# Two of four set-aside attention scores computed and copied in halves of 256 queries

## The chip, the cores and the metric

The kernel runs on one core of one Trainium2 chip. The core has five engines with a queue each, which run side by side and wait for one another through semaphores: TensorE (PE; its weight loads are shown as PEld), VectorE (DVE), ScalarE (ACT), GpSimd (POOL) and SyncE (SP, which here only issues transfers). The metric is the device time of one execution in microseconds (us). PE writes its products to PSUM, a small memory in banks of 512 fp32 values a partition; ACT and DVE read them from there.

## The reference

```python
    def _A_ref(x, wqkv, wo):                     # H = 32 heads of Dh = 16, S = 2048, D = 512
        qkv = (lambda x, *d: x.transpose(*d))((x @ wqkv).reshape(B, S, 3, H, Dh), 2, 0, 3, 1, 4)
        q, k, v = qkv[0], qkv[1], qkv[2]
        scores = jnp.einsum("bhqd,bhkd->bhqk", q, k) * Dh ** -0.5
        p = _softmax(scores, axis=-1)
        o = jnp.einsum("bhqk,bhkd->bhqd", p, v)
        return (lambda x, *d: x.transpose(*d))(o, 0, 2, 1, 3).reshape(B, S, D) @ wo
...
    def _B_ref(x, w1, b1, w2, b2):               # F = 1792
        h = jnp.einsum("bsd,df->bsf", x, w1) + b1
        h = jnp.where(h > 0, h, 0) ** 2
        return jnp.einsum("bsf,fd->bsd", h, w2) + b2
...
    xn = _layernorm(x, axis=-1)
    return x + _A_ref(xn, A_wqkv, A_wo) * _silu(_B_ref(xn, B_w1, B_b1, B_w2, B_b2))
```

So: full attention of 32 narrow heads over 2048 positions, a feed-forward with squared ReLU, and their product (through silu) added to the input, all in fp32.

## The kernel before

After some 150 us of layer norm, transposes and the products for keys, queries and values, the kernel runs a loop of 128 turns (line 754). All of the attention lies in it, and the feed-forward and the output projection are cut into single products that fill the gaps.

**Steps.** A step is one quad of heads (8), one block of 512 queries (4) and one block of 128 keys (16): 512 steps, four to a turn, called i to i+3 in turn n with i = 4n. For each step four heads' scores are wanted, [128 keys, 512 queries] each. They are made in two pairs p = 0, 1 of two heads hp = 0, 1. A score is one product (line 282) of 64 rows: hp = 0 uses PE's rows 0 to 63, hp = 1 rows 64 to 127, so two products run side by side. ACT then takes the exponential of a pair at once (1024 columns, line 286), and four products of 32 columns (line 538, `values`) multiply the exponentials with the values and add them up in the bank `acc`. These come at the end of the turn, 16 products x 2 = 32 of the trace's matmuls for the four steps of a turn.

**Two ways to make a score.** PSUM has eight banks. Four of them are two tiles S of two banks each, used by turns: `scores(i, p)` (line 291) makes a pair in one, and ACT reads it from there. Two banks are `spare`, in which the filling products add up; one is `acc`; and one is `single`, named "lin" in the profile, a tile of [128, 512]. For step i+3 the scores are made in `single`, one head after the other, and set aside: `aside(i, p, hp)` (line 300) makes one product and lets DVE copy it to SBUF, into the place of the exponentials (line 305). ACT later takes the exponential from SBUF in place. So a turn has four set-aside scores, (0,0), (0,1), (1,0), (1,1), called first to fourth here, each of which needs `single` again.

**Filling.** `lin(0)` and `lin(1)` (line 339) each issue one product of 64 rows, lower or upper half, for the block in work; `lin(0, 1)` issues both, which run side by side. A set-aside score is paired with one of them: `lin(0)` stands ahead of a score of hp = 1, `lin(1)` behind one of hp = 0. Blocks come in pairs (`pair`), whose two halves are swapped by `swap()` when the one is done. Most pairs take two turns; the first products of the second feed-forward layer, which are short, take one: the turns with `make and end` (line 766), 8 of 128, called two-pair turns here, where `swap()` stands in the middle of the turn.

**Order.** It is written out by hand (the schedule is manual): each engine runs its instructions in the order of the program, and the library adds the semaphores from what each instruction reads and writes. The branch at line 766 is for two-pair turns, the one at 779 for all the others. In both the second and third set-aside scores stand around the pair scores of step i+2.

At the end (lines 827 to 865) the last rows of the output are made; `two` is one of the S tiles there, whose halves `two[:, 0]` and `two[:, 1]` are used apart: `rest(0, ...)` and `end_rest(0, ...)` in the last turn, `rest(1, ...)` at line 847, `end_rest(1, ...)` at line 861, and `lins[3]`, the last group of line 857, is `two[:, 0]` once more.

Of the kernel before, what the change touches and what calls it, by code (L numbers as in the profile page):

```python
# [46 lines left out]
@with_exitstack  # L47
def mha_ffn_kernel(ctx: ExitStack, tc: tile.TileContext, x, wqkv, wo, bx, w1, b1, w2, b2, out):
    nc = tc.nc
    x, out = x[0], out[0]  # L50
    ctx.enter_context(tc.manual_schedule())
    keep = ctx.enter_context(tc.tile_pool(name="keep", bufs=1))
    dram = ctx.enter_context(tc.tile_pool(name="dram", bufs=1, space=DRAM))

    ident = keep.tile([128, 128], FT, name="ident")
    make_identity(nc, ident)
    vt = keep.tile([128, NK, VW], FT, name="vt")
    nvalid = keep.tile([1, 1], I32, name="nvalid")
    stat = keep.tile([128, 80], FT, name="stat")

    kdram = [[dram.tile([128, 2, 1024], FT, name=f"kd{g}_{h}") for h in range(2)] for g in range(4)]
    qdram = [[dram.tile([128, 2, 512], FT, name=f"qd{g}_{c}") for c in range(NC)] for g in range(4)]
    xdram = [dram.tile([128, 2, 4, 512], FT, name=f"xd{c}") for c in range(3)]

    udram = [[dram.tile([2, 2, 16, 4, 512], FT, name=f"ud{g}_{c}") for c in range(NC)] for g in range(4)]
    zdram = [[dram.tile([4, 512], FT, name=f"zd{q}_{c}") for c in range(NC)] for q in range(NQ)]
    gdram = dram.tile([S, D], FT, name="gd")

    with tc.tile_pool(name="sb", bufs=1) as sb, tc.tile_pool(name="ps", bufs=1, space=PSUM) as ps:
        fast_path(tc, sb, ps, locals())  # L70
    general_path(tc, dram, nvalid, ident, vt, kdram, qdram, gdram, x, wo, out)


def fast_path(tc, sb, ps, env):
# [6 lines left out]
    mm = nc.tensor.matmul  # L81
    dve, act, pool, sp = nc.vector, nc.scalar, nc.gpsimd, nc.sync
# [3 lines left out]
    def t(shape, dt, tag):  # L86

        cnt[0] += 1
        p = ps if tag in ("S", "lin", "acc") else sb
        if tag in BUFS:  # L90
            turn[tag] = turn.get(tag, -1) + 1
            n = turn[tag] % BUFS[tag]
            tag = f"{tag}{places[n] if tag == 'S' else n}"
        return p.tile(shape, dt, tag=tag, name=f"{tag}_{cnt[0]}")
# [180 lines left out]
    steps = [(qd, qc, kb) for qd in range(NQ) for qc in range(NC) for kb in range(NK)]  # L275
    ptile = {}

    def score(i, p, hp, dst):
        qd, qc, kb = steps[i]
        k, q = ka[qd, kb // 8], qa[qd, qc]  # L280
        r = slice(64 * hp, 64 * hp + 64)
        mm(dst, k[r, p, 128 * (kb % 8):128 * (kb % 8) + 128], q[r, p], start=True, stop=True)  # L282

    def exps(i, p, src):
        if src is not None:
            act.activation(ptile[i, p], src, AF.Exp, scale=SCALE)  # L286

    def place(i, p):
        ptile[i, p] = t([128, 2, 512], FT, f"P{2 * ((i - 1) % 4) + p}")

    def scores(i, p):

        if i < len(steps):
            sc = t([128, 2, 512], FT, "S")
            place(i, p)
            for hp in range(2):
                score(i, p, hp, sc[:, hp])
            return sc

    def aside(i, p, hp):  # L300

        if hp == 0:
            place(i, p)
        score(i, p, hp, single)
        dve.tensor_copy(ptile[i, p][:, hp], single)  # L305

    gated, complete, gates = {}, set(), set()

# [30 lines left out]
    def lin(*halves):  # L339
        if pair[0]:  # L340
            for half in halves:
                j = half ^ swapped[0]
                pair[0][j].issue(half, lin_banks[j])

    def swap():
        if pair[0]:
            while any([pair[0][half ^ swapped[0]].issue(half, lin_banks[half ^ swapped[0]]) for half in range(2)]):
                pass
            swapped[0] ^= 1
            if not swapped[0]:  # L350
                pair[0][0].evict()
                pair[0] = None
# [21 lines left out]
    def split_piece(eng=None):  # L374
        if at_piece[1] == len(pieces):
            return
        j, layer, m = pieces[at_piece[1]]
        at_piece[1] += 1
        raw, q = raws.pop(0), PAIRS[m][1]
        wf[layer, m] = [t([128, 4, 256] if layer == 1 else [128, 2, 512], FR, f"wf{layer}{p}{q}") for p in "hl"]  # L380
        split(*wf[layer, m], raw, eng or dve, pool)
        load_piece()
# [149 lines left out]
    def values(i):  # L532
        qd, qc, kb = steps[i]
        if kb == 0:
            acc[0] = t([128, 512], FT, "acc")
        for j in (1, 2, 3, 0) if i % 2 else (0, 1, 2, 3):
            o = (4 * qd + j) * 17
            mm(acc[0][32 * j:32 * j + 32], vt[:, kb, o:o + 32], ptile[i, j // 2][:, j % 2],  # L538
               start=kb == 0, stop=kb == NK - 1)

    def finish(i):

        qd, qc, kb = steps[i]
        if kb < NK - 1:
            return
        if i == len(steps) - 1:
            return
        ou = t([128, 512], FT, "ou")
        cast(act if turn_ends_first[0] else dve, ou, acc[0])
        sp.dma_start(zdram[qd][qc], ou[16::32])  # L550
        for j in range(4):
            sp.dma_start(udram[qd // 2][qc][0, qd % 2, :, j], ou[32 * j:32 * j + 16])
        n = i // 4
        events.setdefault(2 * n + 2, []).insert(0, (load_sums, (qd, qc)))
        at(n + 2, rowsums, qd, qc)
# [174 lines left out]
    def happen(time):  # L730
        for fn, a in events.pop(int(2 * time), ()):
            fn(*a)


    n = turn["S"]
# [4 lines left out]
    single = t([128, 512], FT, "lin")  # L740
    xs[0] = xT[3]

    def rest(i, dst):

        group(dst, lambda p: onorm[2, 3][p][:, cut[i]], lambda p: wos[0][p][:, 3])

    def end_rest(i, src):

        o = t([128, 512], FT, f"wf2{'hl'[i // 2]}{i % 2}")
        dve.scalar_tensor_tensor(o, src, 0.5, gsb[2, i // 2][:, i % 2], op0=OP.mult, op1=OP.mult)  # L750
        pool.dma_start(out[1024 + 128 * i:1152 + 128 * i], o, accum_op=OP.add)

    turn_ends_first = [False]
    for n in range(TURNS):
        i = 4 * n
        happen(n)
        make, end, split_now = fill[n]
        if make:
            pair[0] = make()
        exps(i + 1, 0, scores(i + 1, 0))  # L760
        aside(i + 3, 0, 0)
        lin(1)
        exps(i + 1, 1, scores(i + 1, 1))
        for _ in range(5 if make and end else 4):
            lin(0, 1)
        if make and end:
            lin(0)
            aside(i + 3, 0, 1)
            exps(i + 2, 0, scores(i + 2, 0))
            swap()  # L770
            exps(i + 2, 1, scores(i + 2, 1))
            aside(i + 3, 1, 0)
            lin(1)
            exps(i + 3, 0, ptile[i + 3, 0])
            lin(0, 1)
            last = [scores(i + 4, 0)]
            for _ in range(4):
                lin(0, 1)
        else:
            lin(0)  # L780
            aside(i + 3, 0, 1)
            exps(i + 2, 0, scores(i + 2, 0))
            lin(0, 1)
            lin(0, 1)
            exps(i + 2, 1, scores(i + 2, 1))
            aside(i + 3, 1, 0)
            lin(1)
            exps(i + 3, 0, ptile[i + 3, 0])
            lin(0, 1)
            lin(0, 1)  # L790
            last = [scores(i + 4, 0)]
            lin(0, 1)
            lin(0, 1)
        lin(0)
        aside(i + 3, 1, 1)
        exps(i + 3, 1, ptile[i + 3, 1])
        last.append(scores(i + 4, 1))
        for p in range(2):
            exps(i + 4, p, last[p])
        if n == TURNS - 1:  # L800
            two = t([128, 2, 512], FT, "S")
            rest(0, two[:, 0])
        turn_ends_first[0] = n < LAST and end and fill[n][0] is None and fill[n - 1][2] and n % per in (7, 15, 23)
        swap()
        if n == LAST - 1:
            gsb.update({(2, i): y[2, i] for i in range(2)})
        if n == TURNS - 1:
            end_rest(0, two[:, 0])
        happen(n + 0.5)
        if split_now:  # L810
            split_piece()
        for j in range(4):
            values(i + j)
        finish(i + 3)
# [5 lines left out]
    zc, r = t([128, 16], FT, "zc"), t([128, 16], FT, "rc")  # L820
# [15 lines left out]
    for i in range(4):  # L836
        for j in range(4):
            mm(small[32 * j:32 * j + 32, 0, cut[i]], r[:, 4 * i + j:4 * i + j + 1].broadcast_to([128, 32]), ident,
               start=True, stop=True)
# [138 lines left out]
```

## Time and profile before

| | |
|---|---|
| three runs | 1273.32 us (median), 1272.75 to 1273.88 |
| profiled execution, own time | 1272.96 us |
| its span, first to last instruction | 1271.1 us |
| granted TensorE clock | 0.998 |
| PE, PEld, DVE, ACT, POOL busy | 1257.3, 721.4, 678.5, 1034.2, 257.8 us |
| set-aside products (line 282 into "lin") | 512 |
| their copies (line 305) | 512, 692 ns each |

How to read the lines that follow: the page counts an engine as busy while an instruction of its runs, but PE's matmuls are pipelined and their ends modelled, so 99% is no statement about its peak. A group's line gives the line of the kernel, the engine, the operation, the tiles written <- read (without their numbers), how often, the time in all and the mean in ns; behind the second bar stands how long the engine was idle just before and for whom. The chain of waits follows the work that ended last back from the end; in order of time each piece has its start, its length and what it was. In the timeline a bracket at the end of a row gives the idle time before it and what ended it.

### The profile page before, as it was taken

What the parts mean: (1) busy time and instruction counts of PE and PEld (TensorE: products, weight loads), DVE (VectorE), ACT (ScalarE), POOL (GpSimd) and SP (SyncE); (2) the same over time, 40 slices, a digit from 0 to 9 for tenths busy, and PEclk for the clock granted to TensorE, in tenths of its full rate; (3) what the DMA queues carried; (4) which work ended last, traced back from release to release, by engine and by line L of the source; (5) the groups of instructions that cost most, each with busy time, mean ns of one, the idle gap of its engine ahead of it and who ended that gap; (6) DMA issues with size and microseconds to landing.
All of it is one profiled execution on the core that took longest, in us unless ns stands there. A gap on an engine that the chain in (4) does not pass through costs nothing.

```text
span 1271.1 us, 24788 instructions
## 1 busy us (share of the span) xinstructions
PE 1257.3 (99%) x9925; PEld 721.4 (57%) x9925; DVE 678.5 (53%) x1065; ACT 1034.2 (81%) x1123; POOL 257.8 (20%) x149
## 2 busy tenths in 40 slices
PE   9999999999999999999999999999999999999996
PEld 7888755555555455555555555555555555545553
DVE  5542255455555654545465455555554545566655
ACT  4222588889899898898988889899889988998883
POOL 5000122122211221312022221220331212322111
PEclk9999999999999999999999999999999999999999
DMA  7565513131233132121423222333222132463445
GB/s 266 206 232 197 217 43 102 58 93 59 77 125 109 59 105 64 45 87 48 152 73 109 60 76 60 93 125 108 58 60 87 47 89 59 142 216 125 143 129 118
DMA packets 84940, 137.32 MB, mean 108 GB/s; under 512 B 26058, under 2 KB 40408, under 8 KB 83284
## 3 DMA queue, kind: packets, MB, share of 16 engines
q1 hardware_dynamic: 81668, 126.25, 30.9%
q0 software_dynamic: 2720, 8.65, 2.3%
q8 instruction: 79, 1.29, 0.4%
q10 hardware_dynamic: 432, 0.79, 0.2%
q14 instruction: 41, 0.34, 0.1%
HBM read 94.24 MB, written 41.41 MB: 107 GB/s over the span
## 4 chain that ended last, share of the span: by engine, by line
PE 96%; DVE 2%; ACT 1%; POOL 0%; DMA 0%; issue 0%; ACTq 0%; DVEq 0%
PE acc L538 36%; PE spare L330 26%; PE S L282 16%; PE S L111 9%; PE lin L282 7%; DVE P L305 1%; PE S L204 1%; POOL hl L104 0%; DMA P<-in_A_x_dram 0%; PE acc L111 0%; DVE st L166 0%; DVE P L858 0%; ACT P L286 0%; DVE P L864 0%; ACT wf2h L98 0%
## 5 line engine op out<-in xcount | busy, mean ns | idle before, releaser
L286 ACT ACTIVATE P<-S 128x1024 f32<-128x1024 f32 x768 | 732.4, 1020 | 67.9 <-PE S L282 64.5
L305 DVE COPY P<-lin 128x512 f32<-128x512 f32 x512 | 354.1, 692 | 467.6 <-PE lin L282 342.7
L538 PE MATMUL acc<-P,vt 128*32 128x512 f32 x4096 | 466.0, 595 | 0.0
L282 PE MATMUL S<-QA,KA 64*128 64x512 f32 x1536 | 332.8, 422 | 0.1
L286 ACT ACTIVATE P<-P 128x1024 f32<-128x1024 f32 x256 | 271.4, 1060 | 43.7 <-DVE P L305 43.6
L538 PEld LDWEIGHTS acc<-P,vt 128*32 128x32 f32 x4096 | 120.2, 110 | 272.9 <-issue 272.9
L282 PEld LDWEIGHTS S<-QA,KA 64*128 64x128 f32 x1536 | 145.3, 184 | 159.9 <-ACT P L286 142.6
L282 PE MATMUL lin<-QA,KA 64*128 64x512 f32 x512 | 213.2, 416 | 1.0 <-DVE P L305 0.3
L104 POOL TENSOR_TENSOR wf1l<-wr,wf1h 128x1024 fp32r<-128x1024 f32 x28 | 66.8, 2384 | 404.5 <-DVE wf1h L100 135.3
L330 PE MATMUL spare<-xl,wf1h 64*128 64x512 f32 x504 | 122.3, 400 | 0.0
L104 POOL TENSOR_TENSOR hl<-T,hh 128x1024 fp32r<-128x1024 f32 x28 | 67.6, 2415 | 242.2 <-PE S L282 131.3
L104 POOL TENSOR_TENSOR wf2l<-wr,wf2h 128x1024 fp32r<-128x1024 f32 x28 | 66.7, 2383 | 207.4 <-PE acc L538 139.1
L330 PE MATMUL spare<-wf2l,hh 64*128 64x512 f32 x448 | 107.1, 399 | 0.0
L282 PEld LDWEIGHTS lin<-QA,KA 64*128 64x128 f32 x512 | 94.2, 184 | 22.3 <-DVE P L305 13.6
L330 PE MATMUL spare<-xh,wf1l 64*128 64x512 f32 x504 | 96.3, 392 | 0.0
L330 PE MATMUL spare<-xh,wf1h 64*128 64x512 f32 x504 | 95.5, 390 | 0.0
L330 PE MATMUL spare<-wf2h,hh 64*128 64x512 f32 x448 | 87.7, 392 | 0.0
L330 PE MATMUL spare<-wf2h,hl 64*128 64x512 f32 x448 | 84.6, 391 | 0.0
L330 PEld LDWEIGHTS spare<-xl,wf1h 64*128 64x128 f32 x504 | 67.0, 185 | 8.2
L330 PEld LDWEIGHTS spare<-xh,wf1h 64*128 64x128 f32 x504 | 60.0, 185 | 9.8
L330 PEld LDWEIGHTS spare<-xh,wf1l 64*128 64x128 f32 x504 | 59.8, 185 | 8.4
L98 ACT CAST P<-S 128x512 fp32r<-128x512 f32 x30 | 17.6, 587 | 57.7 <-PE S L111 55.9
(201 smaller groups left out, 995.6 us busy)
## 6 DMA issues: line engine op xcount, KB each, us to landing
wr<-in_B_w_dram SPq DMA_DIRECT2D x56, 512.0 KB
KA<-kd SPq DMA_DIRECT2D x64, 256.0 KB
QA<-qd SPq DMA_DIRECT2D x128, 128.0 KB
kd<-P SPq DMA_DIRECT2D x15, 512.0 KB
qd<-P SPq DMA_DIRECT2D x15, 512.0 KB
u<-ud SPq DMA_DIRECT2D x15, 512.0 KB
P<-in_A_x_dram SPq DMA_DIRECT2D x8, 512.0 KB
xd<-KA SPq DMA_DIRECT2D x4, 1024.0 KB
```

Source lines behind the costliest of these rows:

```text
L98: act.copy(dst, src)
L104: leng.tensor_tensor(lo, src, hi.bitcast(FT), op=OP.subtract)
L111: mm(dst, lhs(a, k), rhs(b, k), start=n == 0, stop=n == len(todo) - 1)
L204: nc.tensor.transpose(pt[:, k, 128 * j:128 * j + 128], xnorm[c, i][:, j, 128 * k:128 * k + 128], ident)
L282: mm(dst, k[r, p, 128 * (kb % 8):128 * (kb % 8) + 128], q[r, p], start=True, stop=True)
L286: act.activation(ptile[i, p], src, AF.Exp, scale=SCALE)
L305: dve.tensor_copy(ptile[i, p][:, hp], single)
L330: mm(bank, self.lhs(a, k)[r], self.rhs(b, k)[r], start=n == 0 and self.at[other] == 0, stop=n == len(self.todo[half]) - 1 and self.at[othe ...
L538: mm(acc[0][32 * j:32 * j + 32], vt[:, kb, o:o + 32], ptile[i, j // 2][:, j % 2], start=kb == 0, stop=kb == NK - 1)
```

## The change

The function `score` gets the columns of the queries as an argument, and `aside_half` makes and copies 256 of the 512 queries of one set-aside score, in the matching half of `single`. The second set-aside score (0,1) is made as two such halves, one right behind the other, in all turns. The third (1,0) is made as two halves too: in ordinary turns the second half stands behind `lin(1)`, in two-pair turns behind `lin(1)` and two `lin(0, 1)`, one of which stood behind ACT's exponential and the other behind `scores(i + 4, 0)`. The first and the fourth stay whole.

```diff
-    def score(i, p, hp, dst):
+    def score(i, p, hp, dst, cols=slice(0, 512)):
         qd, qc, kb = steps[i]
         k, q = ka[qd, kb // 8], qa[qd, qc]
         r = slice(64 * hp, 64 * hp + 64)
-        mm(dst, k[r, p, 128 * (kb % 8):128 * (kb % 8) + 128], q[r, p], start=True, stop=True)
+        mm(dst, k[r, p, 128 * (kb % 8):128 * (kb % 8) + 128], q[r, p, cols], start=True, stop=True)
...
+    def aside_half(i, p, hp, n):
+
+        if hp == n == 0:
+            place(i, p)
+        s = slice(256 * n, 256 * n + 256)
+        score(i, p, hp, single[:, s], s)
+        dve.tensor_copy(ptile[i, p][:, hp, s], single[:, s])
...
         if make and end:
             lin(0)
-            aside(i + 3, 0, 1)
+            for m in range(2):
+                aside_half(i + 3, 0, 1, m)
             exps(i + 2, 0, scores(i + 2, 0))
             swap()
             exps(i + 2, 1, scores(i + 2, 1))
-            aside(i + 3, 1, 0)
+            aside_half(i + 3, 1, 0, 0)
             lin(1)
+            lin(0, 1)
+            lin(0, 1)
+            aside_half(i + 3, 1, 0, 1)
             exps(i + 3, 0, ptile[i + 3, 0])
-            lin(0, 1)
             last = [scores(i + 4, 0)]
-            for _ in range(4):
+            for _ in range(3):
                 lin(0, 1)
         else:
             lin(0)
-            aside(i + 3, 0, 1)
+            for m in range(2):
+                aside_half(i + 3, 0, 1, m)
             exps(i + 2, 0, scores(i + 2, 0))
             lin(0, 1)
             lin(0, 1)
             exps(i + 2, 1, scores(i + 2, 1))
-            aside(i + 3, 1, 0)
+            aside_half(i + 3, 1, 0, 0)
             lin(1)
+            aside_half(i + 3, 1, 0, 1)
             exps(i + 3, 0, ptile[i + 3, 0])
```

## The prediction

> **What bounds the kernel now.** I read the page first: busy times, then the chain that ended last, then the costliest groups.
>
> ```profile
> PE 1257.3 (99%) x9925; PEld 721.4 (57%) x9925; DVE 678.5 (53%) x1065; ACT 1034.2 (81%) x1123; POOL 257.8 (20%) x149
> PE 96%; DVE 2%; ACT 1%; POOL 0%; DMA 0%; issue 0%; ACTq 0%; DVEq 0%
> L286 ACT ACTIVATE P<-S 128x1024 f32<-128x1024 f32 x768 | 732.4, 1020 | 67.9 <-PE S L282 64.5
> L305 DVE COPY P<-lin 128x512 f32<-128x512 f32 x512 | 354.1, 692 | 467.6 <-PE lin L282 342.7
> L538 PE MATMUL acc<-P,vt 128*32 128x512 f32 x4096 | 466.0, 595 | 0.0
> ```
>
> TensorE is the bound: 96% of the chain is its own work. DVE and ACT have room, but what they do counts where PE waits for it. The 4096 value products, 32 a turn, say that there are 128 turns. The next view is the chain of waits inside two of them, in order of time. An ordinary turn (from its second set-aside score on):
>
> ```profile
> 408.36 0.43 PE S L282 x2
> ...
> 410.18 0.23 PE lin L282
> 410.41 0.23 PE S L282 x2
> 410.64 0.46 PE spare L330 x4
> 411.11 0.28 PE S L282 x2
> 411.39 0.33 PE lin L282
> 411.72 0.47 PE spare L330 x5
> ...
> 413.13 0.23 PE S L282 x2
> 413.36 3.57 PE acc L538 x32
> 416.93 0.42 PE S L282
> ```
>
> And a turn in which two output blocks of the feed-forward share the filling (a two-pair turn):
>
> ```profile
> 425.48 0.43 PE S L282 x2
> ...
> 427.53 0.23 PE lin L282
> ...
> 427.84 0.70 DVE P L305
> ...
> 428.58 0.50 PE lin L282
> ...
> 430.84 0.24 PE S L282 x2
> ...
> 434.64 0.42 PE S L282
> ```
>
> A slot, two products side by side in the two halves of PE's rows, takes 0.23 us. The ordinary turn lasts 416.93 - 408.36 = 8.57 us, and PE loses only some 0.15 in it: 0.28 - 0.23 at S, 0.33 - 0.23 at the third set-aside score. The two-pair turn lasts 434.64 - 425.48 = 9.16, and there DVE's copy of the second set-aside score stands in the chain, since the third one's product must wait for the same bank. By the code only 8 of the 128 turns are of this kind (one pair of blocks each, four query blocks of two). So all that the change can win there is 8 x (9.16 - 8.57) = 4.7 us, while it edits two products in all 128 turns.
>
> **The change part by part.** It removes, per turn, two 512-column products into `single` and their two copies, and puts four 256-column products and four 256-column copies in their place. No DMA moves, and nothing is moved past SP's or POOL's queue; ACT's order stays. In two-pair turns one filling slot moves ahead of S(i+4, 0), and the third score's second half stands behind three slots. What decides is one question: `single` is one 128x512 tile; does a product into one half of it wait until DVE has read the other half? The order in program is product, copy, product, copy, so such a wait would put a whole round trip between the halves. The trace has no 256-column piece of this tile, but at the kernel's end two halves of another PSUM tile, `two`, are handled apart: line 861 reads `two[:, 1]` (through line 750), the last group of line 857 then writes `two[:, 0]`, which nobody had read since the last turn. The timeline there, and beside it the chain, where pieces of 256 columns in SBUF go from DVE to ACT:
>
> ```profile
> 1259.94 0.67 DVE L750 SCALAR_TENSOR_TENSOR wf2h<-S,y 128x512 f32<-128x512 f32 x1
> 1260.66 0.30 PEld L664 LDWEIGHTS S<-QA,wf1h 128*128 128x128 f32 x2 [0.56 <-DVE wf2h L750]
> ```
> ```profile
> 1257.05 0.44 DVE P L849
> ...
> 1257.56 0.41 ACT wf1h L850
> ```
>
> PE had nothing else to wait for, and yet it stood 0.56 us until DVE had read the other half: 1259.94 + 0.67 = 1260.61, and 0.05 later it began. In SBUF that isn't so: ACT began the first half at 1257.56 while DVE's second (two of 0.42, row below) was still running. For a tile in PSUM I take the first reading: the halves wait for each other's copies.
>
> The Trainium skill bears on this, in "PSUM — Partial Sum Buffer", section "PSUM bank collisions raise a hardware error": PE may not write a bank and quadrant of partitions while another engine reads it, whatever the columns, so the guard goes by bank. By that rule the two 256-column halves, in one bank of 512, must wait for each other, while `two`'s halves, in two banks, need not; the row shows a wait even there. The rule and the row give the same sum here; the rule speaks against the change.
>
> Price of one round trip, from these rows of the timeline and of the groups:
>
> ```profile
> 408.89 3.80 ACT L286 ACTIVATE P<-S 128x1024 f32<-128x1024 f32 x4 [0.59 <-PE S L282]
> 410.02 0.39 PE L282 MATMUL lin<-QA,KA 64*128 64x512 f32 x1
> 410.48 0.69 DVE L305 COPY P<-lin 128x512 f32<-128x512 f32 x1 [0.66 <-PE lin L282]
> 411.23 0.49 PE L282 MATMUL lin<-QA,KA 64*128 64x512 f32 x1
> ```
> ```profile
> L849 DVE TENSOR_TENSOR P<-S,P 128x256 f32<-128x256 f32 x2 | 0.8, 420 | 1.0 <-PE lin L846 1.0
> L833 DVE COPY zc<-lin 128x16 f32<-128x16 f32 x1 | 0.2, 175 | 0.1
> L282 PEld LDWEIGHTS lin<-QA,KA 64*128 64x128 f32 x512 | 94.2, 184 | 22.3 <-DVE P L305 13.6
> ```
>
> - From product to copy: 410.48 - 410.02 = 0.46 for 512 columns. Half a slot less for 256 (0.46 - 0.115) is 0.35, which I take; the upper end is 0.46.
> - The copy: 692 ns at 512 columns, 175 at 16, so about 0.43 on the line between at 256; line 849 at 256 has 0.42, which I take. The lower end is half of 692, 0.35.
> - From the copy's end (410.48 + 0.69 = 411.17) to PE: 0.06, and 0.05 at `two`. I take 0.05.
> - A product that had to wait shows 0.49 to 0.50 where one that didn't shows 0.39: it streams some 0.11 after its wait is over. The lower end is nothing.
>
> The second half thus streams 0.35 + 0.42 + 0.05 + 0.11 = 0.93 us after the first (0.75 to 1.04). One filling product runs beside the first half; then PE, which issues in order, has everything queued behind the waiting half: S(i+2, 0), the filling, S(i+2, 1). ACT and DVE wait for them in turn.
>
> An ordinary turn by hand, from its second set-aside score as 0. Before, S(i+2, 0) came at 0.23; now it goes beside the second half at 0.93: +0.70. Two filling slots and S(i+2, 1) follow, so PE is at the third score's first half at 0.93 + 4 x 0.23 = 1.85. It needs the copy of the second score's second half, which ends at 0.93 + 0.35 + 0.42 = 1.70, plus 0.05: no new wait, by 0.10. Then comes the second stall of 0.93, and the half behind it takes half a slot to a weight load, 0.115 to 0.184, say 0.13: 0.93 + 0.13 - 0.23 = +0.83. The old 0.15 of waits is covered. Sum +1.38, a turn of 9.95 us. Nothing absorbs it: the eight exponentials at 1.02 make about 8.2 us, they start some 0.55 after their S product as before (408.89 against 408.36), and the two S tiles are free again long before they are wanted; the 3.57 of value products ends the turn as before. DVE has one fixed cost more per split copy, 2 x 0.42 - 0.69 = 0.15, but it stands idle there.
>
> A two-pair turn: half two at 0.93, with it S(i+2, 0), then S(i+2, 1) at 1.16. The third's first half waits for the copy, 1.75 + 0.11 = 1.86 (before, 428.58 + 0.11 - 427.53 = 1.16). Three filling slots, 0.69, don't cover 0.93: the second half at 2.79, S(i+4, 0) at 2.92, three slots and the fourth score, S(i+4, 1) at 4.07 against 430.84 - 427.53 = 3.31 before. +0.76.
>
> Sum: 120 x 1.38 + 8 x 0.76 = 165.6 + 6.1 = 171.7; less some 2 us, an estimate, for the output projections at the end that have 9 instead of 12 products per half and so leave PE room: +170. The profiled execution took 1272.96 us (span 1271.1), the median of the runs is 1273.32, the same within 0.03%: 1272.96 + 170 = **1443 us**. With 0.75 for the round trip a turn costs 1.38 - 2 x 0.18 = 1.02, in all +126: 1399. With 1.04 the third's first half also waits: it comes at 1.04 + 0.92 = 1.96, the copy is done at 1.04 + 0.46 + 0.42 + 0.05 = 1.97, which costs a restart; 1.38 + 2 x 0.11 + 0.12 = 1.72 a turn, in all some +213: 1486.
>
> **The rivals.**
>
> 1. *The halves are kept apart, and it helps.* If a product waits only for its own 256 columns, the third's first half may start when the second's first half is copied, 0.35 + 0.42 + 0.05 = 0.82 after the second score, before PE gets there in an ordinary turn. The 0.10 at 411.39 goes, and at best the whole 0.59 of the two-pair turns: 120 x 0.10 + 8 x 0.59 = 16.7, so 1256 us. For it speaks SBUF, where pieces are kept apart (1257.56); against it the 0.56 us before 1260.66. It decides as soon as nothing waits for the other half.
> 2. *Kept apart, but the weights cost.* Each half loads its own weights: the row says 184 ns, the half streams 115. Two such halves in the same rows need 0.37 instead of 0.23, +0.14 twice a turn: 120 x (0.28 - 0.10) = 21.6, less some 3 in two-pair turns: 1292 us. Between 1 and 2 it may come out even.
> 3. *The stalls chain.* The margin of 0.10 ahead of the third's first half is thin: where DVE is late by more than that, a third wait is added, as worked out above: 1486 or a little more.
>
> That the change doesn't do what it says is my forecast itself: the halves are there, but the second product can't run ahead of the first copy.
>
> The Trainium skill has another figure for rival 2: "TensorE: Matmul & The Clock Gate", section "LDWEIGHTS (loading the stationary operand)", gives columns over 1.2 GHz, 107 ns for 128. By that a load would hide under a half's 115 and rival 2 would cost nothing; the row's 184 decides. My own sum would go down by 0.015 a turn, under 2 us.
>
> **How the numbers follow.** Forecast 0.83; rival 1, 0.06; rival 2, 0.04; an even outcome between them, 0.03; rival 3, 0.04. The time is the forecast's, 1443; the range, 1400 to 1486, is what the bounds of the round trip make it, and takes in rival 3; 0.13 is left out. This kernel's runs can tell 0.2%, 2.5 us, from no change: faster 0.06, same 0.03, slower 0.91.
>
> **What would show it.** In the profile after: four copies of 128x256 at about 0.42 us a turn beside two of 128x512; a turn of some 9.95 us; in the chain DVE's copies twice in every turn, about 256 x 0.42 = 108 us, some 7% of the span; waits of PE on these copies some 256 times, 0.6 us each, where before they came to 13.6 us in all. PE's granted clock stays. I am wrong if a second half's product starts before the first half's copy has ended, or if the turn stays near 8.6 us.

## The result, and the profile after

The changed kernel takes 1461.99 us (median of four runs, 1461.70 to 1462.64) against 1273.49 before (four runs): **1.148 times as long**, 95% interval 1.1466 to 1.1495. The profiled execution took 1462.08 us, its span is 1460.3, the granted clock 0.997. The forecast was 1443 (1400 to 1486).

The page of the changed kernel, its busy times, chain and the groups that are new. Line 313 is the copy in `aside_half`, line 546 the value products:

```profile
PE 1328.5 (91%) x10181; PEld 773.1 (53%) x10181; DVE 718.8 (49%) x1321; ACT 1044.9 (72%) x1123; POOL 257.4 (18%) x149
PE 88%; DVE 9%; issue 2%; POOL 0%; DMA 0%; ACT 0%; DVEq 0%; ACTq 0%
L313 DVE COPY P<-lin 128x256 f32<-128x256 f32 x512 | 217.5, 425 | 283.8 <-PE lin L282 171.4
L282 PEld LDWEIGHTS lin<-QA,KA 64*128 64x128 f32 x768 | 141.0, 184 | 226.3 <-DVE P L313 222.1
```

DVE, 2% of the chain before, is 9% of it now, and what PE's weight loads wait for DVE's copies has gone from 13.6 us to 222.1. DVE's own work rose by only 40 us (678.5 to 718.8). Who waited for whom says it in counts (us in all, times, longest):

```profile
PEld lin L282 <- DVE P L313: 222.1, 268, 1.0
```

268 times is 2 x 128, and a few more. The chain shows where. First an ordinary turn, then a two-pair turn, each from one set of value products to the next:

```profile
458.99 3.57 PE acc L546 x32
462.56 0.43 PE S L282
...
464.69 0.43 DVE P L313
465.12 0.04 issue
465.17 0.38 PE lin L282
...
466.62 0.44 DVE P L313
467.06 0.04 issue
467.10 0.38 PE lin L282
...
469.10 3.57 PE acc L546 x32
```
```profile
475.02 0.44 DVE P L313
475.45 0.04 issue
475.50 0.40 PE lin L282
475.89 0.02 issue
475.91 0.44 DVE P L313
476.35 0.04 issue
476.39 0.38 PE lin L282
476.78 0.58 PE spare L338 x5
...
479.13 3.57 PE acc L546 x32
```

An ordinary turn lasts 469.10 - 458.99 = 10.11 us (8.57 before), with DVE's copy of a half in the chain twice. In the two-pair turn, 479.13 - 469.10 = 10.03 us (9.16 before), the third score's first half waits as well (475.91), and its second half, with three filling slots ahead of it, hardly does. Over all turns, from one turn's first value product to the next's, the mean is 10.09 us in ordinary and 10.05 in two-pair turns (8.58 and 9.15 before): 120 x 1.51 + 8 x 0.90 = 188 us, the whole of the change. The timeline shows one round trip close up. The columns are start, duration, engine, line and operation; the bracket is the idle time before:

```profile
444.03 0.28 PE L282 MATMUL lin<-QA,KA 64*128 64x256 f32 x1
...
444.47 0.42 DVE L313 COPY P<-lin 128x256 f32<-128x256 f32 x1 [0.66 <-PE spare L338]
444.95 0.18 PEld L282 LDWEIGHTS lin<-QA,KA 64*128 64x128 f32 x1 [0.90 <-DVE P L313]
444.95 0.38 PE L282 MATMUL lin<-QA,KA 64*128 64x256 f32 x1 [0.55 <-DVE P L313]
...
445.37 0.42 DVE L313 COPY P<-lin 128x256 f32<-128x256 f32 x1 [0.47 <-PE lin L282]
445.99 0.28 PE L282 MATMUL lin<-QA,KA 64*128 64x256 f32 x1
...
446.40 0.42 DVE L313 COPY P<-lin 128x256 f32<-128x256 f32 x1 [0.60 <-PE lin L282]
446.88 0.18 PEld L282 LDWEIGHTS lin<-QA,KA 64*128 64x128 f32 x1 [0.82 <-DVE P L313]
```

The second half's weights load at 444.95, not before: the copy of the first half ends at 444.47 + 0.42 = 444.89, and 0.06 later PE goes on. PE stood idle 0.55 us: the one filling product that ran beside the first half had ended before that.

### The profile page after: what moved, and what is told of

Read it like the earlier page. It is cut to its first block, busy times and chain, and to the rows that moved or that the text cites. A ratio compares the mean times of both kernels' runs of the same rounds, so it can differ in the third digit from the quotient of the medians.

```text
span 1460.3 us, 25556 instructions
## 1 busy us (share of the span) xinstructions
PE 1328.5 (91%) x10181; PEld 773.1 (53%) x10181; DVE 718.8 (49%) x1321; ACT 1044.9 (72%) x1123; POOL 257.4 (18%) x149
## 4 chain that ended last, share of the span: by engine, by line
PE 88%; DVE 9%; issue 2%; POOL 0%; DMA 0%; ACT 0%; DVEq 0%; ACTq 0%
PE acc L546 31%; PE spare L338 23%; PE S L282 14%; PE lin L282 10%; PE S L111 8%; DVE P L313 8%; PE S L204 0%; POOL hl L104 0%; DMA P<-in_A_x_dram 0%; PE acc L111 0%; DVEq L313 0%; DVE st L166 0%; DVE P L871 0%; POOL wf2l L104 0%; DVE P L877 0%
## 5 line engine op out<-in xcount | busy, mean ns | idle before, releaser
L282 PE MATMUL S<-QA,KA 64*128 64x512 f32 x1536 | 386.5, 418 | 0.0
L282 PE MATMUL lin<-QA,KA 64*128 64x256 f32 (+1 forms) x768 | 271.2, 353 | 117.2 <-DVE P L313 116.7
L313 DVE COPY P<-lin 128x256 f32<-128x256 f32 x512 | 217.5, 425 | 283.8 <-PE lin L282 171.4
L305 DVE COPY P<-lin 128x512 f32<-128x512 f32 x256 | 177.0, 691 | 333.4 <-PE lin L282 212.5
L282 PEld LDWEIGHTS lin<-QA,KA 64*128 64x128 f32 x768 | 141.0, 184 | 226.3 <-DVE P L313 222.1
L282 PEld LDWEIGHTS S<-QA,KA 64*128 64x128 f32 x1536 | 197.8, 184 | 113.4 <-ACT P L286 106.5
L338 PE MATMUL spare<-xh,wf1l 64*128 64x512 f32 x504 | 115.5, 403 | 0.0
L338 PE MATMUL spare<-wf2h,hl 64*128 64x512 f32 x448 | 98.9, 401 | 0.0
L338 PEld LDWEIGHTS spare<-xl,wf1h 64*128 64x128 f32 x504 | 79.5, 185 | 3.5
L338 PEld LDWEIGHTS spare<-wf2l,hh 64*128 64x128 f32 x448 | 70.7, 185 | 2.7
```

The lines of the kernel that those rows point to most:

```text
L313: dve.tensor_copy(ptile[i, p][:, hp, s], single[:, s])
L338: mm(bank, self.lhs(a, k)[r], self.rhs(b, k)[r], start=n == 0 and self.at[other] == 0, stop=n == len(self.todo[half]) - 1 and self.at[othe ...
```

## The experiments

Theory: the halves of one PSUM tile are guarded as one, so each half after the first costs a round trip from PE to DVE and back. Rivals: the second weight load and product, the doubled copies, or a guard that would let the halves pass in another cut. All runs were made beside the kernel before, which took 1273.4 to 1274.2 us there. Unless rounds are told of, a time is that of one run.

### Each split alone

Against the changed kernel, the second alone in halves (in two-pair turns the filling goes back to its places too), then the third alone:

```diff
-            aside_half(i + 3, 1, 0, 0)
+            aside(i + 3, 1, 0)
             lin(1)
-            aside_half(i + 3, 1, 0, 1)
```
```diff
-            for m in range(2):
-                aside_half(i + 3, 0, 1, m)
+            aside(i + 3, 0, 1)
```

> Only the second set-aside score is in halves, the third is whole as before. Theory (a half's product waits for the copy of the half before it, one round trip of 0.9 us a split score): +0.70 for the stall, +0.1 for rows left uneven, less the 0.15 of waits that stand there now: +0.65 a turn, 1273 + 128 x 0.65 = 1356 us. Rival (two products of half the width cost what they cost because each loads its own weights): half of the change's 188, 1367 us, but with no wait on the copy between the halves in the trace.

> Only the third set-aside score is in halves, the second is whole as before. Theory: +0.83 for the stall and some 0.05 for uneven rows, and the small wait ahead of the third's first product stays: +0.85 a turn, 1382 us; with the run of the second alone the two add up to the change's 188 within 15. Rival (weight loads): 1367.

Measured: 1377.59 us and 1375.57 us, +103 and +101 against 1274.17 beside them. The second took 22 us more than expected, the third 6 less; together they make 205, 16 more than the change's 188.5, so "within 15" was just missed. Both show the wait (118.6 us in 136 and 99.6 us in 132 for the weight loads, against 222.1 in 268), so the two stalls are of like size. The times alone don't tell the theory from the rival; the next run does. What the 16 us are isn't shown. Where they lie depends on what one counts from. On the mean over the ordinary turns, from the first product of the pair S(i+4, 0) to the value products it is 1.36 us with the second alone, 1.35 with the third alone, 1.35 with both and 1.27 before, as if 0.08 were lost once, however many scores are split; from the pair's second product it is 1.31, 1.23, 1.23 and 1.25, and no such loss is seen.

### The same products, copied whole

Against the kernel before, with `score` as in the change:

```diff
     def aside(i, p, hp):
...
-        score(i, p, hp, single)
+        if p == hp:
+            score(i, p, hp, single)
+        else:
+            for n in range(2):
+                c = slice(256 * n, 256 * n + 256)
+                score(i, p, hp, single[:, c], c)
         dve.tensor_copy(ptile[i, p][:, hp], single)
```

> The second and third score are made by two products of 256 columns each, one right behind the other, but copied whole, in one copy of 512; all places as before the change. The weight loads and the extra products are those of the change, the round trip between the halves is gone. Theory: uneven rows of 0.1 to 0.15 per split score, partly hidden: 1273 + 128 x (0 to 0.3) = 1273 to 1310 us, no wait on a copy between the halves. Rival (weight loads and extra products are the cost): near the changed kernel, 1440 or more.

Measured: 1273.19 us, where the kernel before took 1274.17. The 768 products into "lin" with their 768 weight loads are all there, as in the changed kernel, and cost nothing that a single run would show; their waits for copies are 6.6 us in all:

```profile
L282 PEld LDWEIGHTS lin<-QA,KA 64*128 64x128 f32 x768 | 129.0, 184 | 21.2 <-DVE P L310 6.6
```

This is the run that decides: take only the copy from between the halves, and 188 us are gone. Rival 2 of the prediction falls, weights and all.

### The same copies, of a whole product

Against the kernel before:

```diff
         score(i, p, hp, single)
-        dve.tensor_copy(ptile[i, p][:, hp], single)
+        for c in ([slice(0, 512)] if p == hp else [slice(0, 256), slice(256, 512)]):
+            dve.tensor_copy(ptile[i, p][:, hp, c], single[:, c])
```

> The kernel before with whole products, but DVE copies the second and third score in two copies of 256 columns each. DVE's part of the change alone, with no product between the copies. Theory: the two copies take 0.85 instead of 0.69 us, so what waits for them waits up to 0.16 longer, at the third score and at ACT's last exponentials: 0 to 0.16 a turn, 1273 to 1295 us. Rival (the doubled copies are the cost): most of the 188 us.

Measured: 1282.47 us, +9 against 1273.42. First a two-pair turn, then an ordinary one, and who waited in all:

```profile
438.59 0.28 PE lin L282
...
438.89 0.77 DVE P L306 x2
```
```profile
457.04 0.29 PE S L282 x2
457.34 0.39 PE lin L282
```
```profile
PEld lin L282 <- DVE P L306: 30.2, 127, 0.7
```

The two copies take 0.77 together where one took 0.70 (427.84). The two-pair turn had that copy in its chain before, and these turns are no longer than they were (9.15 us on the mean). An ordinary turn's chain has no copy in it; there the third score, whose weights wait a little longer for the pair of copies (30.2 us in all, before 13.6), stands 0.39 in the chain where it stood 0.33 (411.39), and 120 times the 0.06 are 7 of the 9 us.

So neither the products alone (0) nor the copies alone (9) make the 188; their order, product, copy, product, copy, does.

### How coarse the guard is: halves by keys

Against the changed kernel (`score` takes 64 keys instead of 256 queries):

```diff
+        if keys < 128:
+            kw, qw = kw.bitcast(FT), qw.bitcast(FT)
...
-        s = slice(256 * n, 256 * n + 256)
-        score(i, p, hp, single[:, s], s)
-        dve.tensor_copy(ptile[i, p][:, hp, s], single[:, s])
+        s = slice(64 * n, 64 * n + 64)
+        score(i, p, hp, single[s], 64 * n, 64)
+        dve.tensor_copy(ptile[i, p][s, hp], single[s])
```

> The same places as in the changed kernel, but the halves are 64 keys by 512 queries: they lie on different partitions (0 to 63, 64 to 127) of the bank instead of different columns. Their products run in plain fp32, which takes two passes, 0.45 us a half instead of 0.115, and each copy is 64x512, about 0.69. It tells how coarse the wait is. Theory that the whole tile is guarded: the second half's product starts only after the first's copy has ended, a round trip of some 1.5 us, twice a turn: near 1700 us. Rival that the guard goes by the bank and its partitions: the second half follows the first at once, while the first is being copied; only the dearer products count, some +1.35 a turn, near 1445 us.

Measured: 2113.02 us, above both. Its timeline:

```profile
620.84 1.07 PE L285 MATMUL lin<-QA,KA 64*64 64x512 f32 x2
621.94 0.68 DVE L316 COPY P<-lin 64x512 f32<-64x512 f32 x1 [1.63 <-PE lin L285]
622.68 0.19 PEld L285 LDWEIGHTS lin<-QA,KA 64*64 64x64 f32 x2 [1.66 <-DVE P L316]
622.68 1.07 PE L285 MATMUL lin<-QA,KA 64*64 64x512 f32 x2 [0.78 <-DVE P L316]
```

The time is no measure: a half's product took 1.07 us, not the 0.45 that I had put in. The order is: the second half, on other partitions, began at 622.68, 0.06 after the first's copy had ended (621.94 + 0.68). So the guard isn't one by partitions either. With the wait at `two`, whose halves are in different banks, this says that in this kernel a PSUM tile is guarded as a whole, by the semaphores that the library adds. Whether the chip itself would allow such an overlap wasn't tried: there was no ninth bank to give the halves tiles of their own.

### The round trip's terms: what stands ahead of the half, and what stands behind it

Against the changed kernel, the filling product behind the second score's first half (in both kinds of turns), then two more slots between the third's halves (in ordinary turns):

```diff
-            lin(0)
-            for m in range(2):
-                aside_half(i + 3, 0, 1, m)
+            aside_half(i + 3, 0, 1, 0)
+            lin(0)
+            aside_half(i + 3, 0, 1, 1)
```
```diff
             aside_half(i + 3, 1, 0, 0)
             lin(1)
+            lin(0, 1)
+            lin(0, 1)
             aside_half(i + 3, 1, 0, 1)
             exps(i + 3, 0, ptile[i + 3, 0])
-            lin(0, 1)
-            lin(0, 1)
```

> The changed kernel with the filling product lin(0) of the second score issued behind its first half instead of ahead of it; nothing else differs. In the changed kernel the first half's copy starts 0.44 us after the product, not the 0.35 of the prediction. Theory: the half's end is held by the 512-column product ahead of it on PE; now that is gone, the copy starts 0.35 after, 0.09 a turn less: 1462 - 11 = 1451 us. Rival (the time from product to copy doesn't depend on the columns or the neighbour): 1462, still 0.44.

Measured: 1445.12 us, 17 less than the changed kernel's 1462 where 11 were expected. The half and its copy:

```profile
440.10 0.27 PE L282 MATMUL lin<-QA,KA 64*128 64x256 f32 x1
440.41 0.42 DVE L313 COPY P<-lin 128x256 f32<-128x256 f32 x1 [0.52 <-PE lin L282]
```

0.31 us from the product to its copy, where the changed kernel has 0.44 and names the filling product ("PE spare") as what the copy waited for. So the half's end was held by the 512-column product issued just ahead of it.

> The changed kernel, but in ordinary turns too the third score's second half stands behind lin(1) and both lin(0, 1), as the change has it in two-pair turns. No work is added or taken. Theory (the cost is a round trip in which PE only stands still, so work placed into it is free): 0.46 of the third's 0.93 is filled; the fourth score then comes 0.82 after the second half and must wait some 0.1 to 0.2 for its copy, so 0.26 to 0.46 a turn are saved: 1407 to 1431 us. Rival (the cost is work on PE or DVE): 1462.

Measured: 1418.79 us, in the range: 43 less with the same work in another order. Time that can be filled with other work was waiting, not work. In the chain the second stall is gone:

```profile
436.29 0.70 PE spare L338 x5
436.99 0.30 PE lin L282
437.29 0.23 PE S L282 x2
```

### More pieces

> Only the second score by two products of 256 columns, copied whole; the third by one. Both split scores together cost nothing when copied whole (1273), while each alone as halves cost more (103 and 101 us) than half of the two together (188). Theory: two products in one half of PE's rows leave it some 0.1 us behind the other half; the second does that to the rows 64 to 127, the third to the rows 0 to 63, so together they are even and alone they aren't: 128 x (0.06 to 0.13), 1281 to 1290 us. Rival (the rows don't matter): 1273.

The edit is that of the run with whole copies, for the second score alone. Measured: 1271.89 us against 1273.66, in three rounds, ratio 0.9988 (0.9979 to 0.9998): two products in one half of the rows cost nothing when they are copied whole, and with that my theory for the 16 us falls. What causes them stays open.

Last, the second score alone in quarters, against the run with it alone in halves:

```diff
-            for m in range(2):
+            for m in range(4):
                 aside_half(i + 3, 0, 1, m)
...
-        s = slice(256 * n, 256 * n + 256)
+        s = slice(128 * n, 128 * n + 128)
```

> Only the second score, in four quarters of 128 queries, each copied by itself; the third whole. Theory (every piece after the first adds one round trip): the first takes 0.42 to its copy, about 0.29 for a copy of 128 columns (on the line through 175 ns at 16 and 425 at 256) and 0.05, in all 0.76; the two behind it 0.11 + 0.25 + 0.29 + 0.05 = 0.70 each; the last streams 0.11 after its wait: 2.27 us from the first product to S(i+2, 0), against 1.03 with halves. +1.24 a turn over the run with the second alone in halves, 1378 + 159 = 1536 us. Rival (the cost goes by the columns handled apart, which are the same 512): 1378.

Measured: 1589.11 us, 53 above. Its chain, an ordinary turn:

```profile
456.32 3.57 PE acc L546 x32
...
461.99 0.30 DVE P L313
462.33 0.34 PE lin L282
462.70 0.30 DVE P L313
...
463.04 0.34 PE lin L282
463.40 0.30 DVE P L313
...
463.75 0.33 PE lin L282
...
466.96 3.57 PE acc L546 x32
```

Three copies in the chain, 0.71 apart (462.33, 463.04, 463.75 against the 0.70 worked out), and a turn of 10.64 us; with the second score in halves it is 9.39, so +1.25 against the +1.24 expected. The price of a round trip holds; the 53 us come from something else, the last section.

### A better order?

Against the kernel before, in ordinary turns:

```diff
-            lin(0, 1)
-            lin(0, 1)
+            for _ in range(3):
+                lin(0, 1)
             exps(i + 2, 1, scores(i + 2, 1))
             aside(i + 3, 1, 0)
             lin(1)
             exps(i + 3, 0, ptile[i + 3, 0])
-            lin(0, 1)
             lin(0, 1)
```

> Not the change but the kernel before, all scores whole; in ordinary turns one lin(0, 1) moves from behind the third score to ahead of S(i+2, 1). By the trace of before PE loses 0.05 at S(i+2, 1) and 0.10 at the third score of such a turn. Theory: both waits are covered, and the fourth score, whose copy of the third must be done by then, costs back 0.1 at most: 120 x (0 to 0.15), 1256 to 1274 us. Rival (the exponentials bound the turn too, ACT is just as late): 1273, the same.

Measured: 1275.80 us against 1273.42 in five rounds, ratio 1.0018 (1.0009 to 1.0027): no gain. The third score's wait is gone (PE's weight loads waited 6.2 us for copies, before 13.6), and an ordinary turn takes 8.61 us on the mean, before 8.58. So the 0.10 at the third score was no loss that a better place would win back. The wait has moved to S(i+4, 0), which now comes sooner than ACT has freed its tile:

```profile
412.18 0.19 PEld L282 LDWEIGHTS S<-QA,KA 64*128 64x128 f32 x2 [0.23 <-ACT P L286]
```

It waits so in all 118 ordinary turns between the first and the last of the loop, in the kernel before in 9 of them, while S(i+2, 1) waited for ACT in 115 there. That is what the rival said: the exponentials are just as late. None of the runs beats the kernel before by more than 0.2%.

## Why the prediction was right

- **The bound, and what can be won.** Right: PE sets the turn, and the stall of the two-pair turns is a small target. It wasn't even won: these turns grew from 9.15 to 10.05 us.
- **The decisive reading.** Right, and shown: from the wait at `two` the prediction took it that halves of a PSUM tile wait for each other's copies. Whole copies (1273), the timeline (444.95) and the halves by keys all say the same. The Trainium skill's "PSUM — Partial Sum Buffer", section "PSUM bank collisions raise a hardware error", forbids the overlap in one bank and quadrant; the guard seen here is coarser than that rule, as it also held between partitions 0 to 63 and 64 to 127.
- **The round trip.** 0.93 forecast. Copy 0.425 (0.42 forecast), copy to PE 0.06 (0.05), restart 0.10 to 0.11 (0.11): right. From product to copy I had 0.35; it is 0.31 with nothing in the way (440.10 to 440.41, and 0.42 after a restart), but 0.44 and 0.41 in the changed kernel. This term was mis-sized: I subtracted half a slot for the shorter product and forgot that it comes behind a long one (shown for the 0.44; for the 0.41 it wasn't tried apart). 0.09 + 0.06 = 0.15 a turn.
- **An ordinary turn.** +1.38 forecast, 10.11 - 8.57 = +1.54 in the turn shown. The mean is +1.53 up to the last 16 turns and +1.40 in those, which have the output projections; 16 x 0.13 are the 2 us that the forecast took off there. The 0.15 make up the difference; that the third score's first half wouldn't wait, by a margin of 0.10, held (445.99 has no bracket). Not all of the old 0.15 of waits was covered: S(i+2, 1) still takes 0.28 in the chain (466.25).
- **A two-pair turn.** +0.76 forecast, +0.87 measured in the turn shown, +0.90 on the mean. The third's first half waits as forecast (475.91); that the rest is the same term is argued, not shown.
- **The sum.** 1443 forecast, 1462 measured: 120 x 0.15 = 18 us of the 19 missing.
- **Rival 1** (the halves are free of each other) never came about, since nothing passes the guard. **Rival 2** costs nothing that the runs show: a weight load that the row gives 184 ns is hidden although the half streams for 115, both alone (1271.9) and for both scores (1273.2). **Rival 3** didn't come: a third wait is seen in the 8 two-pair turns only, where the forecast itself had it.
- **What would show it.** Two copies in the chain of each turn, 256 waits and an unchanged clock came as said; the waits were longer or shorter than the 0.6 us each, by what one counts: 222 us by the weight loads (0.83 each, of which part passes beside the neighbour's product), 117 by the products (0.47).

## What to carry to other kernels

Cutting a piece of work in two to free its buffer earlier can help only if the halves are tracked apart; where the buffer is guarded as one, each cut adds a whole round trip between the engines, product to copy to product, and the engine that issues in order stands still for all of it that isn't filled with other work. Look for a place in the trace where two parts of such a buffer are already used apart, and read there whether anyone waited. And count the turns: a stall in 8 of 128 doesn't pay for an edit in all.

## What was not expected of the hardware

PE's clock. In the changed kernel, which pauses twice a turn, and in all others but two it was granted in full over the whole loop (0.997 or 0.998 over the span). With three pauses in a row (the quarters) it was halved in the loop 33 times, for 3.41 us each. The busy times around one of them, windows of the quarters' run; the columns are busy us and count of each engine, then PEclk:

```profile
151.61:155.02 3.41, 2.26 (x16) 1.83 (x18) 1.17 (x4) 1.11 (x2) 0.00 (x0) 1.00 0.96 259
155.03:158.43 3.40, 3.40 (x19) 2.39 (x19) 1.46 (x3) 2.11 (x4) 0.00 (x0) 0.50 0.92 350
```

PE was busy for 2.26 of 3.41 us, 66%, in the stretch ahead, and the next one ran at half clock. The changed kernel's emptiest stretch of that length kept the full clock with 72%:

```profile
444.00:447.40 3.40, 2.46 (x20) 1.65 (x19) 1.37 (x4) 2.57 (x3) 0.00 (x0) 1.00 0.71 191
```

At half the clock half of each such stretch is lost: 33 x 3.41 / 2 = 56 us, near the 53 that the quarters took beyond the forecast. The halves by keys, at a granted clock of 0.935, have halved stretches too, but ahead of one of them, at 201.54, PE was busy for 88%:

```profile
198.12:201.53 3.41, 2.99 (x11) 0.83 (x9) 0.85 (x2) 2.58 (x3) 0.00 (x0) 1.00 0.00 0
```

So the busy share alone isn't what decides, and what does stays open. The Trainium skill, "TensorE: Matmul & The Clock Gate", Part 1, describes a window of 3413 ns and a clock that is either full or half, which fits; its table names an idle window as what halves it, and here a window two thirds busy was enough.
